# Decode attention on one core: a third halving on VectorE for half of each tile, and the Values matmuls in a hardware loop on TensorE

## The chip, the core and the metric

The kernel runs on one core of a Trainium2 chip. Five engines work side by side[...]: TensorE (PE, matmuls into PSUM), VectorE (DVE), ScalarE (ACT), GpSimd (POOL) and SyncE (SP), which here issues the loads. Sixteen DMA engines carry the loads. The metric is the time on the device in microseconds (us).

## The reference

One query per head attends to 4,096 keys: 8 batches of 32 heads, head dimension D = 128, all in bfloat16.

```python
B, H, Sq, Skv, Dh = 8, 32, 1, 4096, 128
def reference(q, k, v):
    scale = q.shape[-1] ** -0.5
    scores = jnp.einsum('bhqd,bhkd->bhqk', q, k) * scale
    attn = _softmax(scores, axis=-1)
    return jnp.einsum('bhqk,bhkd->bhqd', attn, v)
```

K and V are 268 MB each, and every element is used once.

## The kernel before

**Tiles.** A tile is 8 heads; there are 32 tiles (NT). One tile of K or V is 128 partitions x 256 positions (C) x 128 (D) in bfloat16, 8.39 MB. Sixteen partitions hold one head, each with 256 of its positions.

**Scores of a tile.** `q_prep` (lines 156 to 168) spreads the queries of the 8 heads over the partitions, with two small matmuls and two copies on ScalarE. `product` (170) works on units of 64 positions, four to a tile: VectorE multiplies K by the query in place (175), then adds the upper half of D to the lower (178), so that 64 of 128 remain. `sum_over_d` (185) lets PE add these up: with an identity as weights, eight matmuls of 512 columns accumulate into one bank of PSUM, each taking 8 values of D (DS) for 64 positions. `scores_of` (199) reduces the last 8 on VectorE. `weights_of` (209) finds the maximum and a bias per head (212 to 223), and ScalarE computes the eight exponentials (231), one for each head, with the row sums. For each head, the bias outside its own 16 partitions is so low that the weights there are zero.

**Values.** `values_of` (241) multiplies the weights by V: 64 matmuls (256), each with 4 positions x 8 heads = 32 columns of weights and 4 x 128 = 512 columns of V. They go round four groups of 32 output rows (`group`, TG = 4). `copy_of` (280) brings the result from PSUM to SBUF on ScalarE; `result_of` (289) picks the matching rows and sums them on PE (301), two tiles into one bank; `norm_of`, `recip_of` and `finish_of` divide by the sum and store. Every eight tiles, ScalarE issues an output DMA.

**Buffers.** K has two buffers, V has one (`KB, VB = 2, 1`). The last tile's V uses a K buffer. A load into a buffer waits until the last reader of the former tile is done: for V that is the last Values matmul, for K the last matmul of `sum_over_d`.

**Order.** Everything stands in the order in which the program is written (`manual_schedule`). In iteration t, SP gets the load of K of t + 1 and then V of t. PE gets the sums of units 0 and 1 of tile t, then the Values of tile t - 1, then the sums of units 2 and 3, then the pick of t - 1. VectorE gets the four units in turn, each unit's last reduce one unit later, and the maxima at the end. For the last two tiles the Values stand behind all four sums. Each engine takes its instructions strictly in this order.

**Cuts.** Some loads are issued in pieces (`cuts`, line 131): K of tile 0 as a quarter, a quarter and a half, with the load of the queries behind the first quarter; K of the last four tiles in halves (or a quarter, a quarter and a half), V of the last tile in seven pieces.

Of the kernel before, what the change touches and what calls it, by code (L numbers as in the profile page):

```python
# [7 lines left out]
ACT = mybir.ActivationFunctionType  # L8
ALU = mybir.AluOpType
AX = mybir.AxisListType  # L10
BF16 = mybir.dt.bfloat16
F32 = mybir.dt.float32

G = 8
KB, VB = 2, 1
TG = 4
R = 2
OB = 4
LAST = 4
NEG = -1.0e30  # L20


@with_exitstack
def kernel(
# [7 lines left out]
    nc = tc.nc  # L32
    B, H, Sq, D = q.shape
    S = k.shape[2]
    P = nc.NUM_PARTITIONS
# [3 lines left out]
    C = S // PH  # L39
    NT = NH // G  # L40
    scale = float(D) ** -0.5
    UC = 64
    DS = 512 // UC
    NU = C // UC
    MC = UC
    CB = 4
    RG = R * G
    NQ = NT // R
    TB = 32
    AG = CB * G  # L50
    assert TG * AG == P and NH % P == 0 and P % G == 0 and TB % PH == 0 and C % CB == 0

    q_n = q.rearrange("b h o d -> (b h o) d").rearrange("(x p) d -> p x d", p=P)
# [13 lines left out]
    ps_v = ctx.enter_context(tc.tile_pool(name="ps_v", bufs=2, space=bass.MemoryType.PSUM))  # L67
# [42 lines left out]
    for j in range(TG):  # L110
# [17 lines left out]
    nc.gpsimd.memset(w_last[:], 0.0)  # L128

    loads = {}  # L130
    cuts = {
        ("k", 0): [C // 4, C // 4, C // 2],
        ("k", NT - 4): [C // 2] * 2,
        ("k", NT - 3): [C // 2] * 2,
        ("k", NT - 2): [C // 2] * 2,
        ("k", NT - 1): [C // 4, C // 4, C // 2],
# [3 lines left out]
    def load(kind, t):  # L140
        src = k_t if kind == "k" else v_t
        home = "v" if kind == "v" and t < NT - 1 else "k"
        pool = k_pool if home == "k" else v_pool
        buf = pool.tile([P, C, D], BF16, name=f"{kind}t", tag=home)
        c0 = 0
        for n in cuts.get((kind, t), [C]):
            nc.sync.dma_start(buf[:, c0 : c0 + n, :], src[t, :, c0 : c0 + n, :])  # L147
            c0 += n
            if kind == "k" and t == 0 and c0 == n:
                nc.sync.dma_start(q_all[:], q_n)  # L150
        assert c0 == C
        loads[kind, t] = buf
# [3 lines left out]
    def q_prep(t):  # L156
        x, p0 = divmod(t * G, P)
        qh = ps_q.tile([G, D], F32, name="qh", tag="qp")
        nc.tensor.matmul(  # L159
            qh[:], lhsT=ident[:, p0 : p0 + G], rhs=q_all[:, x, :], start=True, stop=True  # L160
        )
        qg = q_pool.tile([G, D], BF16, name="qg", tag="qg")
        nc.scalar.activation(out=qg[:], in_=qh[:], func=ACT.Copy)  # L163
        qp = ps_q.tile([P, D], F32, name="qp", tag="qp")
        nc.tensor.matmul(qp[:], lhsT=heads[:].rearrange("g h x -> g (h x)"), rhs=qg[:], start=True, stop=True)  # L165
        qb = q_pool.tile([P, 1, D], BF16, name="qb", tag="qb")
        nc.scalar.activation(out=qb[:, 0, :], in_=qp[:], func=ACT.Copy)  # L167
        qbs[t] = qb

    def product(t, lo, hi):  # L170
        kt = loads["k", t]
        qb = qbs[t]
        for c0 in range(lo, hi, MC):
            part = kt[:, c0 : c0 + MC, :]
            nc.vector.tensor_tensor(  # L175
                out=part, in0=part, in1=qb[:].to_broadcast([P, MC, D]), op=ALU.mult
            )
            nc.vector.tensor_tensor(  # L178
                out=part[:, :, 0 : D // 2], in0=part[:, :, 0 : D // 2],
                in1=part[:, :, D // 2 : D], op=ALU.add,  # L180
            )

    sums = {}

    def sum_over_d(t, u):
        kt = loads["k", t]
        ps = ps_s.tile([P, UC, DS], F32, name="ps", tag="ps")
        n = D // 2 // DS
        for s in range(n):
            nc.tensor.matmul(  # L190
                ps[:], lhsT=ident[:],
                rhs=kt[:, u * UC : (u + 1) * UC, s * DS : (s + 1) * DS],
                start=(s == 0), stop=(s == n - 1),
            )
        sums[t, u] = ps
# [3 lines left out]
    def scores_of(t, u):  # L199
        if u == 0:  # L200
            scs[t] = sc_pool.tile([P, C], F32, name="sc", tag="sc")
        nc.vector.tensor_reduce(  # L202
            out=scs[t][:, u * UC : (u + 1) * UC], in_=sums.pop((t, u))[:], axis=AX.X, op=ALU.add
        )

    ws = {}
# [30 lines left out]
            nc.gpsimd.tensor_copy(out=w_last[:, :, RG - G : RG], in_=w[:, C - LAST : C, :])  # L237

    avs = {}

    def values_of(t, lo, hi):
        vt = loads["v", t]
        w = ws[t]
        if lo == 0:
            avs[t] = ps_v.tile([P, CB * D], F32, name="av", tag="av")
        end = C if t < NT - 1 else C - LAST


        group = [
            0 if t == NT - 1 and C // 2 <= c0 < 3 * C // 4 else c0 // CB % TG  # L250
            for c0 in range(0, end, CB)
        ]
        for c0 in range(lo, hi, CB):
            i = c0 // CB
            j = group[i]
            nc.tensor.matmul(  # L256
                avs[t][j * AG : (j + 1) * AG, :], lhsT=w[:, c0 : c0 + CB, :],
                rhs=vt[:, c0 : c0 + CB, :], start=(i < TG), stop=(j not in group[i + 1 :]),
            )

    ops = {}
# [4 lines left out]
    def norm_of(n):  # L266
        zp = ps_z.tile([RG, 1], F32, name="zp", tag="zp")
        nc.tensor.matmul(  # L268
            zp[:], lhsT=esums.pop(n).rearrange("p r g -> p (r g)"), rhs=ones[:],
            start=True, stop=True,  # L270
        )
        zps[n] = zp

    def recip_of(n):
        rzs[n] = small.tile([RG, 1], F32, name="rz", tag="rz")
        nc.vector.reciprocal(out=rzs[n][:], in_=zps.pop(n)[:])  # L276
# [3 lines left out]
    def copy_of(t):  # L280
        comb = small.tile([P, CB, D], BF16, name="comb", tag="comb")
        av = avs.pop(t)[:].rearrange("p (m d) -> p m d", d=D)
        n = CB if t < NT - 1 else CB // 2
        nc.scalar.activation(out=comb[:, 0:n, :], in_=av[:, 0:n, :], func=ACT.Copy)  # L284
        if n < CB:
            nc.vector.tensor_copy(out=comb[:, n:CB, :], in_=av[:, n:CB, :])  # L286
        combs[t] = comb

    def result_of(t):
        n, r = divmod(t, R)  # L290
        comb = combs.pop(t)
        if r == 0:
            ops[n] = ps_o.tile([RG, D], F32, name="op", tag="op")
        if t == NT - 1:
            for i in range(LAST):
                nc.tensor.matmul(
                    ops[n][:], lhsT=w_last[:, i, :], rhs=loads["v", t][:, C - LAST + i, :],
                    start=False, stop=False,
                )
        for m in range(CB):  # L300
            nc.tensor.matmul(  # L301
                ops[n][:], lhsT=pick[:, m, r, :], rhs=comb[:, m, :],
                start=(r == 0 and m == 0), stop=(r == R - 1 and m == CB - 1),
            )

    def finish_of(n):
        s, u = divmod(n, OB)
        if u == 0:
            stages[s] = o_pool.tile([RG, OB, D], BF16, name="stage", tag="stage")
        nc.scalar.activation(  # L310
            out=stages[s][:, u, :], in_=ops.pop(n)[:], func=ACT.Copy, scale=rzs.pop(n)[:, 0:1]
        )
        last = s == NQ // OB - 1
        if u == OB - 1 or (last and u == OB - 2):
            lo = u if (last and u == OB - 1) else 0
            nc.scalar.dma_start(o_n[s, :, lo : u + 1, :], stages[s][:, lo : u + 1, :])

    Q = C // 4
    load("k", 0)
    with tc.manual_schedule():  # L320
        q_prep(0)
        for t in range(NT):
            v_last = t >= NT - 2
            n = t // R - 1
            if t + 1 < NT:
                load("k", t + 1)
            load("v", t)
            product(t, 0, Q)
            sum_over_d(t, 0)
            if t > 2 and t % R == 1:  # L330
                recip_of(n)
                finish_of(n)
            if t + 1 < NT:
                q_prep(t + 1)
            product(t, Q, 2 * Q)
            sum_over_d(t, 1)
            scores_of(t, 0)
            if t > 0 and not v_last:
                values_of(t - 1, 0, C)
                copy_of(t - 1)  # L340
            product(t, 2 * Q, 3 * Q)
            sum_over_d(t, 2)
            scores_of(t, 1)
            product(t, 3 * Q, C)
            sum_over_d(t, 3)
            scores_of(t, 2)
            if t > 0 and v_last:
                values_of(t - 1, 0, C)
            scores_of(t, 3)
            weights_of(t)  # L350
            if t > 0:
                if v_last:
                    copy_of(t - 1)
                if t % R == 0:
                    norm_of(n)
                result_of(t - 1)
        values_of(NT - 1, 0, C // 2)
        norm_of(NQ - 1)
        recip_of(NQ - 1)
        values_of(NT - 1, C // 2, C - LAST)  # L360
        copy_of(NT - 1)
        result_of(NT - 1)
        finish_of(NQ - 1)

# [29 lines left out]
```

## Time and profile before

| what | value |
|---|---|
| median of 10 runs | 1254.55 us (1254.4 to 1254.77) |
| the profiled execution | 1254.51 us, span 1252.8 us |
| bytes read | 536.94 MB, 429 GB/s over the span |
| VectorE busy | 967.5 us (77%) |
| PE matmuls busy | 550.7 us (44%) |
| ScalarE busy | 343.3 us (27%) |
| granted TensorE clock, mean | 0.688 |
| instruction fetches on queue q8 | 26 packets, 0.43 MB |

The span runs from the first to the last instruction of the core. In a line of groups, the columns are line, engine, operation, output and inputs, shapes, count, then the busy time in us and the mean ns of one, then the engine's idle time ahead of them and what ended most of it. In a line of the timeline, the start and the duration come first, and the bracket gives the idle time before and its releaser. In the chain of work that ended last, each line has start, duration and what ran or was waited for. PE's clock is granted by a throttle: 1.00 is full speed.

### The profile page before, as it was taken

The numbers are of one execution on the slowest core, as the hardware profiler recorded it, in microseconds if no ns is written. First come the engines' busy times: TensorE is split into PE (matmuls) and PEld (weight loads), VectorE is DVE, ScalarE is ACT, GpSimd is POOL, SyncE is SP. The second block draws the span as 40 slices with busy tenths as digits, with TensorE's granted clock in tenths as the row PEclk, the third lists the DMA queues.
The fourth block names the chain that finished last, engine by engine and source line by source line (L and its number), as shares of the span: only waits on it lengthen the run. The fifth ranks groups of instructions, "written<-read, shape, count | busy, mean of one in ns | idle before, by whom it ended". The sixth has DMA issues, their size and how long they took to land.

```text
span 1252.8 us, 8134 instructions
## 1 busy us (share of the span) xinstructions
PE 550.7 (44%) x3299; PEld 201.3 (16%) x3299; DVE 967.5 (77%) x531; ACT 343.3 (27%) x625; POOL 6.0 (0%) x26
## 2 busy tenths in 40 slices
PE   2444543445533355333554344543345424544355
PEld 0111111111111111111111111111111101111112
DVE  6877887777977779777797777886778877977981
ACT  0333123332133321333213333123330233321333
POOL 1000000000000000000000000000000000000000
PEclk9966756776666676667675667656677566766677
DMA  9999999999999999999999999999999999999997
GB/s 404 435 436 432 434 435 435 434 432 432 435 434 431 434 432 427 435 434 433 432 434 434 432 436 435 434 434 435 429 427 433 432 435 434 423 426 433 429 440 311
DMA packets 11734, 537.53 MB, mean 429 GB/s; under 512 B 1840, under 2 KB 2096, under 8 KB 2352
## 3 DMA queue, kind: packets, MB, share of 16 engines
q1 hardware_dynamic: 11360, 536.94, 99.3%
q8 instruction: 26, 0.43, 0.1%
q10 hardware_dynamic: 336, 0.07, 0.0%
q14 instruction: 12, 0.10, 0.0%
HBM read 536.94 MB, written 0.07 MB: 429 GB/s over the span
## 4 chain that ended last, share of the span: by engine, by line
DMA 79%; PE 15%; DVE 6%; issue 0%; another core or an unknown queue 0%; ACT 0%; SPq 0%
DMA vt<-in_v_dram 78%; PE av L256 13%; DVE kt L175 3%; DVE kt L178 2%; PE ps L190 1%; DMA q_all<-in_q_dram 1%; DVE sc L202 0%; SPq L147 0%; DVE pmax L212 0%; DVE spread L214 0%; DVE nmax L219 0%; DVE comb L286 0%; ACT comb L284 0%; ACT stage L310 0%
## 5 line engine op out<-in xcount | busy, mean ns | idle before, releaser
L175 DVE TENSOR_TENSOR kt<-kt,qb 128x8192 bf16<-128x8192 bf16 x128 | 565.1, 4415 | 185.2 <-DMA kt<-in_k_dram 178.5
L190 PE MATMUL ps<-kt,ident 128*128 128x512 bf16 x1024 | 351.8, 506 | 573.3 <-DVE kt L178 573.3
L231 ACT ACTIVATE w<-sc,bias 128x256 bf16<-128x256 f32 x256 | 300.5, 1587 | 255.4 <-DVE bias L223 255.4
L178 DVE TENSOR_TENSOR kt<-kt 128x4096 bf16<-128x4096 bf16 x128 | 293.3, 2292 | 4.4
L190 PEld LDWEIGHTS <-ident 128*128 128x128 bf16 x1024 | 118.9, 118 | 776.5 <-issue 502.7
L256 PE MATMUL av<-vt,w 128*32 128x512 bf16 x2047 | 175.6, 510 | 88.3 <-DMA vt<-in_v_dram 88.3
L202 DVE TENSOR_REDUCE sc<-ps 128x64 f32<-128x512 f32 x128 | 87.6, 685 | 65.6 <-PE ps L190 65.6
L284 ACT ACTIVATE comb<-av 128x512 bf16<-128x512 f32 (+1 forms) x32 | 19.5, 609 | 415.3 <-PE av L256 415.3
L231 ACT ACTIVATION_READ_ACCUMULATOR w<-sc,bias 128x1 f32 x256 | 126.5, 494 | 0.0
L256 PEld LDWEIGHTS <-w 128*32 128x32 bf16 x2047 | 68.3, 124 | 204.7 <-DMA vt<-in_v_dram 107.2
L163 ACT ACTIVATE qg<-qh 8x128 bf16<-8x128 f32 x32 | 8.5, 267 | 167.8 <-PE qh L159 167.8
L310 ACT ACTIVATE stage<-op,rz 16x128 bf16<-16x128 f32 x16 | 6.0, 372 | 57.5 <-DVE rz L276 42.8
L301 PE MATMUL op<-comb,pick 128*16 128x128 bf16 x128 | 13.1, 226 | 16.5 <-ACT comb L284 16.1
L212 DVE TENSOR_REDUCE pmax<-sc 128x1 f32<-128x256 f32 x32 | 13.4, 420 | 1.1
L165 PE MATMUL qp<-qg,heads 8*128 8x128 bf16 x32 | 7.6, 238 | 12.7 <-ACT qg L163 12.7
L276 DVE RECIPROCAL rz<-zp 16x1 f32<-16x1 f32 x16 | 2.4, 149 | 14.0 <-PE zp L268 14.0
L159 PE MATMUL qh<-q_all,ident 128*8 128x128 bf16 x32 | 8.2, 256 | 8.5 <-DMA q_all<-in_q_dram 8.5
L167 ACT ACTIVATE qb<-qp 128x128 bf16<-128x128 f32 x32 | 8.9, 278 | 10.4 <-PE qp L165 10.4
L301 PEld LDWEIGHTS <-pick 128*16 128x16 bf16 x128 | 7.5, 90 | 24.2 <-issue 24.0
L214 DVE TENSOR_SCALAR spread<-same,pmax 128x32 f32<-128x32 f32 x32 | 7.7, 241 | 1.1
L223 DVE TENSOR_SCALAR bias<-own,nmax 128x8 f32<-128x8 f32 x32 | 7.4, 231 | 1.1
L219 DVE TRANSPOSE_TENSOR_REDUCE nmax<-spread 128x1 f32<-128x32 f32 x32 | 6.8, 212 | 1.1
(27 smaller groups left out, 20.2 us busy)
## 6 DMA issues: line engine op xcount, KB each, us to landing
kt<-in_k_dram SPq DMA_DIRECT2D x8, 4096.0 KB, 43.5
kt<-in_k_dram SPq DMA_DIRECT2D x4, 2048.0 KB, 22.8
vt<-in_v_dram SPq DMA_DIRECT2D x1, 4096.0 KB, 41.7
vt<-in_v_dram SPq DMA_DIRECT2D x1, 2048.0 KB, 46.2
vt<-in_v_dram SPq DMA_DIRECT2D x1, 1024.0 KB, 48.1
vt<-in_v_dram SPq DMA_DIRECT2D x1, 512.0 KB, 48.9
vt<-in_v_dram SPq DMA_DIRECT2D x31, 33.4
kt<-in_k_dram SPq DMA_DIRECT2D x27, 47.4
```

Source lines behind the costliest of these rows:

```text
L159: nc.tensor.matmul(qh[:], lhsT=ident[:, p0 : p0 + G], rhs=q_all[:, x, :], start=True, stop=True)
L163: nc.scalar.activation(out=qg[:], in_=qh[:], func=ACT.Copy)
L167: nc.scalar.activation(out=qb[:, 0, :], in_=qp[:], func=ACT.Copy)
L175: nc.vector.tensor_tensor(out=part, in0=part, in1=qb[:].to_broadcast([P, MC, D]), op=ALU.mult)
L178: nc.vector.tensor_tensor(out=part[:, :, 0 : D // 2], in0=part[:, :, 0 : D // 2], in1=part[:, :, D // 2 : D], op=ALU.add,)
L190: nc.tensor.matmul(ps[:], lhsT=ident[:], rhs=kt[:, u * UC : (u + 1) * UC, s * DS : (s + 1) * DS], start=(s == 0), stop=(s == n - 1),)
L202: nc.vector.tensor_reduce(out=scs[t][:, u * UC : (u + 1) * UC], in_=sums.pop((t, u))[:], axis=AX.X, op=ALU.add)
L212: nc.vector.tensor_reduce(out=pmax[:], in_=sc[:], axis=AX.X, op=ALU.max)
L231: nc.scalar.activation(out=w[:, :, g], in_=sc[:], func=ACT.Exp, bias=bias[:, g : g + 1], scale=scale, accum_out=esum[:, t % R, g : g + 1],)
L256: nc.tensor.matmul(avs[t][j * AG : (j + 1) * AG, :], lhsT=w[:, c0 : c0 + CB, :], rhs=vt[:, c0 : c0 + CB, :], start=(i < TG), stop=(j not i ...
L284: nc.scalar.activation(out=comb[:, 0:n, :], in_=av[:, 0:n, :], func=ACT.Copy)
L301: nc.tensor.matmul(ops[n][:], lhsT=pick[:, m, r, :], rhs=comb[:, m, :], start=(r == 0 and m == 0), stop=(r == R - 1 and m == CB - 1),)
```

## The change

Four edits are made.

1. For units 0 and 1 of each tile up to tile 28, VectorE adds once more, so that 32 of 128 values of D remain, and PE takes four matmuls for such a unit instead of eight (`width_of`).
2. K of tile 0 is loaded in two halves, with the queries behind the first half; K of tile 28 (NT - 4) is loaded in one piece.
3. The last copy out of PSUM is done by ScalarE alone; before, ScalarE and VectorE took half each. In the last tile, 12 instead of 16 matmuls of the second half go to row group 0.
4. The Values of tiles 0 to 30 are computed by `values_loop`: two matmuls, then a hardware loop on PE of ten rounds with six matmuls each whose addresses come from registers, then two more. All 64 go to one group of 32 rows. The loop is a critical section: PE waits at its entry for what stands ahead of it in the program, and drains at its end. The copy and the pick read 32 partitions instead of 128. The loads of K of t + 1 and V of t, and the products, are ordered behind the loop that precedes them; this orders the program and adds no semaphore.

```diff
-        ("k", 0): [C // 4, C // 4, C // 2],
-        ("k", NT - 4): [C // 2] * 2,
+        ("k", 0): [C // 2] * 2,
...
+    def width_of(t, u):
+        return D // 4 if u < NU // 2 and t < NT - 3 else D // 2
...
+            if width_of(t, c0 // UC) < D // 2:
+                nc.vector.tensor_tensor(
+                    out=part[:, :, 0 : D // 4], in0=part[:, :, 0 : D // 4],
+                    in1=part[:, :, D // 4 : D // 2], op=ALU.add,
+                )
...
-        n = D // 2 // DS
+        n = width_of(t, u) // DS
...
+    def values_loop(t):
+        vf = loads["v", t][:].rearrange("p c d -> p (c d)")
+        wf = ws[t][:].rearrange("p c g -> p (c g)")
+        avs[t] = ps_v.tile([P, CB * D], F32, name="av", tag="av")
+        av = avs[t][0:AG, :]
+        nv, nw = CB * D, CB * G
+        def one(i, **how):
+            pe.matmul(
+                av, lhsT=wf[:, i * nw : (i + 1) * nw], rhs=vf[:, i * nv : (i + 1) * nv], **how
+            )
+        with tc.tile_critical() as loop:
+            for i in range(EDGE):
+                one(i, start=(i == 0), stop=False)
+            end = (NV - EDGE) * nw
+            pe.reg_mov(rw, EDGE * nw)
+            pe.reg_mov(rv, EDGE * nv)
+            with pe.While(lambda: pe.snap(rw, min_val=EDGE * nw, max_val=end) < end):
+                ow = pe.snap(rw, min_val=EDGE * nw, max_val=end - LOOP * nw)
+                ov = pe.snap(rv, min_val=EDGE * nv, max_val=(NV - EDGE - LOOP) * nv)
+                for i in range(LOOP):
+                    pe.matmul(
+                        av, lhsT=wf[:, bass.ds(ow + i * nw, nw)],
+                        rhs=vf[:, bass.ds(ov + i * nv, nv)],
+                        start=False, stop=False,
+                    )
+                pe.reg_add(rw, rw, LOOP * nw)
+                pe.reg_add(rv, rv, LOOP * nv)
+            for i in range(NV - EDGE, NV):
+                one(i, start=False, stop=(i == NV - 1))
+        loops.append(loop)
...
-            0 if t == NT - 1 and C // 2 <= c0 < 3 * C // 4 else c0 // CB % TG
+            0 if t == NT - 1 and C // 2 <= c0 < C // 2 + 3 * C // 16 else c0 // CB % TG
...
-        n = CB if t < NT - 1 else CB // 2
-        nc.scalar.activation(out=comb[:, 0:n, :], in_=av[:, 0:n, :], func=ACT.Copy)
-        if n < CB:
-            nc.vector.tensor_copy(out=comb[:, n:CB, :], in_=av[:, n:CB, :])
+        n = P if t == NT - 1 else AG
+        nc.scalar.activation(out=comb[0:n, :, :], in_=av[0:n, :, :], func=ACT.Copy)
...
+    def before_values(t):
+        v_last = t >= NT - 2
...
+        product(t, Q, 2 * Q)
+        sum_over_d(t, 1)
+        scores_of(t, 0)
+        if v_last:
+            products_end(t)
...
+    def after_values(t):
...
+        if t > 0 and not v_last:
+            copy_of(t - 1)
+        if t + 1 < NT:
+            load("k", t + 1)
+        load("v", t)
+        if not v_last:
+            products_end(t)
+        scores_of(t, 3)
+        weights_of(t)
...
         for t in range(NT):
...
             if t > 0:
+                after_values(t - 1)
+            before_values(t)
+            if t > 0:
+                values_loop(t - 1)
+        after_values(NT - 1)
```

`NV` is 64, `EDGE` 2 and `LOOP` 6. `products_end` holds the units 2 and 3 with their sums and reduces.

More of the change, by code (lines that the diff above doesn't have):

```diff
@@ L19 @@
 LAST = 4
+LOOP = 6
+EDGE = 2
 NEG = -1.0e30
@@ L50 @@
     AG = CB * G
+    NV = C // CB
+    assert (NV - 2 * EDGE) % LOOP == 0
     assert TG * AG == P and NH % P == 0 and P % G == 0 and TB % PH == 0 and C % CB == 0
@@ L130, with behind_loop @@
     loads = {}
+    loops = []
+    def behind_loop(made):
+        if loops:
+            tc.add_manual_dep(
+                made.ins, loops[-1].name,
+                mybir.DependencyInfo(
+                    mybir.DependencyClass.NoSync, mybir.DependencyReason.SCHED_ONLY
+                ),
+            )
     cuts = {
-        ("k", 0): [C // 4, C // 4, C // 2],
-        ("k", NT - 4): [C // 2] * 2,
+        ("k", 0): [C // 2] * 2,
         ("k", NT - 3): [C // 2] * 2,
@@ L146, in load @@
         for n in cuts.get((kind, t), [C]):
-            nc.sync.dma_start(buf[:, c0 : c0 + n, :], src[t, :, c0 : c0 + n, :])
+            dma = nc.sync.dma_start(buf[:, c0 : c0 + n, :], src[t, :, c0 : c0 + n, :])
+            behind_loop(dma)
             c0 += n
@@ L174, in product @@
             part = kt[:, c0 : c0 + MC, :]
-            nc.vector.tensor_tensor(
+            made = nc.vector.tensor_tensor(
                 out=part, in0=part, in1=qb[:].to_broadcast([P, MC, D]), op=ALU.mult
             )
+            behind_loop(made)
             nc.vector.tensor_tensor(
@@ L239 @@
     avs = {}
+    pe = nc.tensor
+    rv = pe.alloc_register("rv")
+    rw = pe.alloc_register("rw")
+    def values_loop(t):
[22 more added lines that the diff above has]
+                        start=False, stop=False,
+                    )
+                pe.reg_add(rw, rw, LOOP * nw)
[3 more added lines that the diff above has]
+        loops.append(loop)
     def values_of(t, lo, hi):
@@ L299, in result_of @@
                 )
+        e = P if t == NT - 1 else AG
         for m in range(CB):
             nc.tensor.matmul(
-                ops[n][:], lhsT=pick[:, m, r, :], rhs=comb[:, m, :],
+                ops[n][:], lhsT=pick[0:e, m, r, :], rhs=comb[0:e, m, :],
                 start=(r == 0 and m == 0), stop=(r == R - 1 and m == CB - 1),
@@ L318, with products_end @@
     Q = C // 4
+    def before_values(t):
+        v_last = t >= NT - 2
+        n = t // R - 1
+        if t == 0:
+            q_prep(0)
+        product(t, 0, Q)
+        sum_over_d(t, 0)
+        if t > 2 and t % R == 1:
+            recip_of(n)
+            finish_of(n)
+        if t + 1 < NT:
+            q_prep(t + 1)
+        product(t, Q, 2 * Q)
[3 more added lines that the diff above has]
+            products_end(t)
+    def products_end(t):
+        product(t, 2 * Q, 3 * Q)
+        sum_over_d(t, 2)
+        scores_of(t, 1)
+        product(t, 3 * Q, C)
+        sum_over_d(t, 3)
+        scores_of(t, 2)
@@ L319 @@
+    def after_values(t):
+        v_last = t >= NT - 2
+        if t > 0 and not v_last:
+            copy_of(t - 1)
+        if t + 1 < NT:
+            load("k", t + 1)
[5 more added lines that the diff above has]
+        if t > 0:
+            if v_last:
+                copy_of(t - 1)
+            if t % R == 0:
+                norm_of(t // R - 1)
+            result_of(t - 1)
     load("k", 0)
-    with tc.manual_schedule():
-        q_prep(0)
+    E = mybir.EngineType
@@ L322 @@
+    with tc.manual_schedule(engines={E.PE, E.DVE, E.Activation, E.SP}):
         for t in range(NT):
[L323 to L350, printed above, removed]
-            if t > 0:
[L352 to L356, printed above, removed]
+            if t > 0:
+                after_values(t - 1)
@@ L357 @@
+            before_values(t)
+            if t > 0:
+                values_loop(t - 1)
+        after_values(NT - 1)
         values_of(NT - 1, 0, C // 2)
```

## The prediction

> **What bounds the kernel now.** I read the page's shares first, then the chain that ended last in order of time, then one period of the timeline, then clock and durations of single stretches. The page:
>
> ```profile
> span 1252.8 us, 8134 instructions
> DMA  9999999999999999999999999999999999999997
> HBM read 536.94 MB, written 0.07 MB: 429 GB/s over the span
> DMA 79%; PE 15%; DVE 6%; issue 0%; another core or an unknown queue 0%; ACT 0%; SPq 0%
> L256 PE MATMUL av<-vt,w 128*32 128x512 bf16 x2047 | 175.6, 510 | 88.3 <-DMA vt<-in_v_dram 88.3
> q8 instruction: 26, 0.43, 0.1%
> ```
>
> The transfers are full in every slice; chain and bytes agree that K and V set the time. The chain in order of time shows how it closes, once per tile:
>
> ```profile
> 567.78 5.35 PE av L256 x64
> 573.15 33.50 DMA vt<-in_v_dram
> 606.66 0.04 issue
> 606.70 6.50 PE av L256 x63
> 613.21 32.01 DMA vt<-in_v_dram
> 645.22 0.04 issue
> 645.27 5.35 PE av L256 x64
> ```
>
> Period 645.27 - 606.70 = 38.6 us, two 8.39 MB loads. V has one buffer, so a V load can be issued only when the Values of the tile before are done; it then still waits some 32 us, most of it queued behind the K load. That queueing is the cover. K and V take 19.3 us each, so after V lands at 606.7 the next K lands at 626 and only then is the next V needed, about 2 us of issue ahead: Values may end as late as 624 and end at 613.2. The compute of one period:
>
> ```profile
> 606.70 6.46 PE L256 MATMUL av<-vt,w 128*32 128x512 bf16 x64 [2.42 <-DMA vt<-in_v_dram]
> 613.09 1.90 PE L190 MATMUL ps<-kt,ident 128*128 128x512 bf16 x8
> 618.85 0.23 DVE L223 TENSOR_SCALAR bias<-own,nmax 128x8 f32<-128x8 f32 x1
> 625.97 4.43 DVE L175 TENSOR_TENSOR kt<-kt,qb 128x8192 bf16<-128x8192 bf16 x1 [6.88 <-DMA kt<-in_k_dram]
> 630.43 2.29 DVE L178 TENSOR_TENSOR kt<-kt 128x4096 bf16<-128x4096 bf16 x1
> 632.77 3.57 PE L190 MATMUL ps<-kt,ident 128*128 128x512 bf16 x8 [15.34 <-DVE kt L178]
> ```
>
> VectorE has only 6.9 us of slack before K. Clock in stretches (columns: stretch, length, PE busy, granted clock, DMA share, GB/s):
>
> ```profile
> 606.70:613.10 6.40, 6.40 (x65) 0.55 1.06 461
> 1193.00:1196.50 3.50, 3.50 (x67) 1.00 1.04 445
> 613.10:615.00 1.90, 1.89 (x12) 1.00 1.04 448
> 593.99:597.50 3.51, 3.51 (x9) 0.50 0.95 411
> ```
>
> At full clock 64 Values take 3.5 us (55 ns each) but eight L190 matmuls, also 512 columns, take 1.90 us (216 ns each after the tail), 3.5 us at half clock: the 64 Values run four abreast.
>
> [...]
>
> **The change, part by part.**
>
> *Values loop (31 tiles).* All 64 matmuls go to one 32-row group, so nothing runs abreast: 64 x 0.216 = 13.8 us at full clock against 3.5. Cold start: Values now take 5.2 to 6.5 us against 3.5, so half clock adds 1.7 to 3.0; I take 2.0. [...] Register work: seven address instructions and one move an iteration, unpriced. [...] Let X be the loop's time[...].
>
> *What X feeds.* In PE's order, sums of the second half of the same tile stand behind the loop. From loop end E: drain 0.3, sixteen L190 at full clock 3.65, last reduce, maxima and bias to the next product 1.87 (1193.04 to 1194.91 in the timeline): E + 5.8. Then the first half of the next tile's products: 6.67 per unit now (625.97 to 632.64), plus the new halving of 2,048 elements, half of L178's 4,096: 1.17, so 2 x 7.84 = 15.7: E + 21.5. Four cold sums 1.88 and the entry's waits 0.1: the next loop starts at E + 23.5. So a period is **X + 23.5**, and it beats the transfers' 38.7 from X = 15.2 up. At 17.4 it is 40.9. V independently needs E + 2 + 19.4 = E + 21.4, just inside. ScalarE's exps (9.4 us after bias) are inside too. The four sums fewer per unit save 1.7 us on this path; the halving costs 2.3: net +0.6, included. The other four sums saved lie beside the products.
>
> *Entry waits.* The loop waits for all that stands ahead of it in the program: mostly long done, but in tiles 9, 17 and 25 also an output DMA that ScalarE issues after its exps at about E + 15.6, which lands 14.3 us later (its row of issues), so 6.4 late. Behind it are the loop, the sums and VectorE's reduce. 3 x 6.4 = 19 us (0 if it lands quickly).
>
> *Start.* K's first load in halves is 4.19 MB ahead of q_all instead of 2.1: q_all lands 4.85 us later and the first product starts at 14.6 instead of 9.7. Tile 0 also halves twice (2.3): the first loop starts at 68.1, against 61.8. Were transfers still the limit, this would be hidden behind K0, K1, V0 (58 us); with computing the limit it counts.
>
> *End.* Tiles 29 to 31 keep the old halving. After loop 28's end E: products of tile 30 27.9 us from E + 5.8, sums 3.4, loop 29 from E + 37.3. Only its end frees V's buffer, when K31 has long landed; V30 lands 21.5 later; loop 30 starts at E + 58.8 + X and ends X later; the rest of tile 31, output included, about 10: E + 68.8 + 2X = E + 103.6.
>
> *Beside other work or nothing.* [...] The copy of 32 rows streams the same columns (0.62 us), on ScalarE's idle time. The last copy whole: 0.62 for 0.39 + 0.44, 0.2 saved; last tile's group 12 matmuls wide instead of 16: about 0.6 saved. K28 in one piece instead of halves: hidden while computing is behind.
>
> **Sum**, against the profiled execution: 68.1 + 28 x 40.9 + 17.4 + 103.6 + 19 = 1353 us of span. Launch around the span adds 1.7 (1254.51 against 1252.8; the median of the runs, 1254.55, is the same): **1355**. Every us of X is worth 31.
>
> **Rivals.** (1) *A slow loop.* Register instructions or a clock that stays half while only a quarter of the columns work: X = 20 to 28, 1355 + 31 x 2.6 = 1436 to 1684. For: no such instruction is in this trace, and the granted clock was 0.55 through 606 to 613. Against: it rose to 1.00 in bursts of continuous work. (2) *Transfers stay the limit.* If X is at most 15.2 the period stays 38.7. Then only the end shows: loop 28 ends 9 us later than now, loop 29 takes 14 instead of 3.6, V30 is issued at 1216 instead of 1197 while K31 lands at 1208: 10 us idle, 1256 to 1272. Against: it needs 13.8 plus almost no cold time. (3) *Faster.* 26 instruction blocks become about 14[...]. If all of them went through one of the 16 DMA engines, 12 x 16 KiB at 27 GB/s free it 7 us: 1247 to 1250. It decides only if the loop stays within 15.2 and V30's gap is covered, which the end argues against; the 0.1% of all engines says less than 1 us if spread.
>
> **Chances.** X between 15.2 and 20, transfers no longer the limit: 0.56 (own range 1285 to 1436). Slow loop: 0.30, of it 0.08 above 1610. Transfers the limit, paying at the end: 0.07. No measurable change: 0.02. Faster: 0.05. About 0.2% is what a measurement of this kernel can tell from no change. The range 1262 to 1610 holds the first case, most of the second and part of the third. Faster 0.05, same 0.02, slower 0.93.
>
> **What would show it.** Right: the chain mostly PE and VectorE; the loop's line near 17 us per tile, matmuls 216 ns or more apart; VectorE waiting on PE's sums instead of K; DMA below 9 in the slices; loop starts 41 us apart, 47 in tiles 9, 17 and 25; fewer instruction packets. Wrong: a loop under 15 us with VectorE still waiting for K (rival 2 or 3), or matmuls over 300 ns apart (rival 1). A loop whose matmuls overlap, or sums that need not queue behind it, would undo the argument.

## The result and the profile after

| | before | after |
|---|---|---|
| median of the runs | 1254.52 us (1254.37 to 1255.89) | 1358.4 us (1355.7 to 1360.86) |
| ratio, 95% interval | | 1.0828 [1.0818, 1.0837] |
| the profiled execution | 1254.51 us, span 1252.8 us | 1355.1 us, span 1353.4 us |
| rate over the span | 429 GB/s | 397 GB/s |
| granted TensorE clock, mean | 0.688 | 0.769 |

The kernel is 8.3% slower; the execution that the profiler took was the fastest of its ten. On the page of the changed kernel, the lines that answer to those shown of before:

```profile
span 1353.4 us, 11319 instructions
...
DMA  9989999999998999999997999999999899999683
...
q8 instruction: 14, 0.23, 0.1%
HBM read 536.94 MB, written 0.07 MB: 397 GB/s over the span
...
L217 PE MATMUL ps<-kt,ident 128*128 128x512 bf16 x792 | 253.7, 476 | 483.3 <-DVE kt L205 427.8
L294 PE MATMUL av<-vt,w 128*32 x1860 | 457.9, 403 | 3.3
```

The transfers are no longer full in every slice; instruction blocks fell from 26 to 14; the Values' line, which had waited 88.3 us for V, shows no wait for V any more (run 5 tells why that is not quite the whole story). The page's chain of what ended last is of no use here: it goes back only to the drain of the last loop. The period has to be read from the timeline of PE (start, duration, what; in brackets the idle time before and its releaser):

```profile
640.84 1.04 PE L280 MATMUL av<-vt,w 128*32 128x512 bf16 x2 [0.44 <-issue]
641.67 14.78 PE L294 MATMUL av<-vt,w 128*32 x60
656.51 0.61 PE L280 MATMUL av<-vt,w 128*32 128x512 bf16 x2
657.31 3.61 PE L217 MATMUL ps<-kt,ident 128*128 128x512 bf16 x16 [0.20 <-PEq L284]
660.85 0.39 PE L364 MATMUL op<-comb,pick 32*16 32x128 bf16 x4
670.86 1.86 PE L217 MATMUL ps<-kt,ident 128*128 128x512 bf16 x4 [9.62 <-DVE kt L205]
672.65 0.27 PE L175 MATMUL qh<-q_all,ident 128*8 128x128 bf16 x1
673.34 0.26 PE L181 MATMUL qp<-qg,heads 8*128 8x128 bf16 x1 [0.41 <-ACT qg L179]
678.78 1.86 PE L217 MATMUL ps<-kt,ident 128*128 128x512 bf16 x4 [5.18 <-DVE kt L205]
681.08 1.04 PE L280 MATMUL av<-vt,w 128*32 128x512 bf16 x2 [0.44 <-issue]
```

The Values take 640.84 to 657.11, 16.3 us where they took 5.3 to 6.5 in the tiles shown of before; the next loop starts 24.0 us after that end. VectorE in the same period:

```profile
650.70 2.29 DVE L200 TENSOR_TENSOR kt<-kt 128x4096 bf16<-128x4096 bf16 x1
659.23 0.69 DVE L229 TENSOR_REDUCE sc<-ps 128x64 f32<-128x512 f32 x1 [6.24 <-PE ps L217]
...
662.80 4.42 DVE L196 TENSOR_TENSOR kt<-kt,qb 128x8192 bf16<-128x8192 bf16 x1
667.26 2.29 DVE L200 TENSOR_TENSOR kt<-kt 128x4096 bf16<-128x4096 bf16 x1
669.58 1.22 DVE L205 TENSOR_TENSOR kt<-kt 128x2048 bf16<-128x2048 bf16 x1
```

Its wait moved: 6.9 us for K before, 6.2 us for PE's sums now, and the next product starts without any wait.

Time after against time before, by parts: the first loop starts 6.9 us later (68.66 against 61.8), the stretch from first to 29th Values takes 1148.7 us instead of 1088.3, the 29th Values take 10.1 us longer (16.27 against 6.13), and from there to the end it is 119.7 us instead of 96.6.

### The profile page after: what moved, and what is told of

Its sections match the earlier page's. It is cut to its first block, busy times and chain, and to the rows that moved or that the text cites. A ratio compares the mean times of both kernels' runs of the same rounds, so it can differ in the third digit from the quotient of the medians.

```text
span 1353.4 us, 11319 instructions
## 1 busy us (share of the span) xinstructions
PE 788.2 (58%) x3067; PEld 298.5 (22%) x3067; DVE 1038.1 (77%) x588; ACT 341.4 (25%) x625; POOL 6.0 (0%) x26
## 5 line engine op out<-in xcount | busy, mean ns | idle before, releaser
L217 PE MATMUL ps<-kt,ident 128*128 128x512 bf16 x792 | 253.7, 476 | 483.3 <-DVE kt L205 427.8
L294 PE MATMUL av<-vt,w 128*32 x1860 | 457.9, 403 | 3.3
L294 PEld LDWEIGHTS av<-vt,w 128*32 x1860 | 188.4, 101 | 279.2 <-issue 119.6
L217 PEld LDWEIGHTS <-ident 128*128 128x128 bf16 x792 | 85.5, 110 | 620.9 <-issue 568.7
L348 ACT ACTIVATE comb<-av 32x512 bf16<-32x512 f32 (+1 forms) x32 | 18.8, 587 | 738.0 <-PEq L284 731.9
L280 PE MATMUL av<-vt,w 128*32 128x512 bf16 x124 | 50.8, 502 | 48.1 <-DMA out_dram<-stage 17.9
L205 DVE TENSOR_TENSOR kt<-kt 128x2048 bf16<-128x2048 bf16 x58 | 71.0, 1224 | 2.0
L340 DVE RECIPROCAL rz<-zp 16x1 f32<-16x1 f32 x16 | 2.4, 150 | 39.5 <-PE zp L332 39.5
L280 PEld LDWEIGHTS av<-vt,w 128*32 128x32 bf16 x124 | 7.7, 101 | 90.4 <-issue 89.8
L364 PE MATMUL op<-comb,pick 32*16 32x128 bf16 (+1 forms) x128 | 12.3, 215 | 1.7 <-ACT comb L348 1.7
L364 PEld LDWEIGHTS <-pick 32*16 32x16 bf16 (+1 forms) x128 | 6.7, 83 | 9.0 <-issue 8.6
## 6 DMA issues: line engine op xcount, KB each, us to landing
vt<-in_v_dram SPq DMA_DIRECT2D x1, 512.0 KB, 39.5
vt<-in_v_dram SPq DMA_DIRECT2D x31, 22.1
```

Of the source, the lines that this page charges most:

```text
L205: nc.vector.tensor_tensor(out=part[:, :, 0 : D // 4], in0=part[:, :, 0 : D // 4], in1=part[:, :, D // 4 : D // 2], op=ALU.add,)
L217: nc.tensor.matmul(ps[:], lhsT=ident[:], rhs=kt[:, u * UC : (u + 1) * UC, s * DS : (s + 1) * DS], start=(s == 0), stop=(s == n - 1),)
L280: pe.matmul(av, lhsT=wf[:, i * nw : (i + 1) * nw], rhs=vf[:, i * nv : (i + 1) * nv], **how)
L294: pe.matmul(av, lhsT=wf[:, bass.ds(ow + i * nw, nw)], rhs=vf[:, bass.ds(ov + i * nv, nv)], start=False, stop=False,)
L348: nc.scalar.activation(out=comb[0:n, :, :], in_=av[0:n, :, :], func=ACT.Copy)
L364: nc.tensor.matmul(ops[n][:], lhsT=pick[0:e, m, r, :], rhs=comb[0:e, m, :], start=(r == 0 and m == 0), stop=(r == R - 1 and m == CB - 1),)
```

## The experiments

**1. Is it the loop, or the work added on VectorE?** Everything of the change but the loop:

```diff
-                values_loop(t - 1)
+                values_of(t - 1, 0, C)
```

(with the copy and the pick over 128 partitions again).

> Everything of the change except the hardware loop: the Values are again 64 static matmuls that go round four groups of 32 rows; the smaller adds, the cuts and the last copy stay changed. Theory (the loop's length and what queues behind it on PE set the time): Values take 5 to 6.5 us, the period is the transfers' 38.7 us again, the 2.4 us of added halving and the later start of the first product vanish in VectorE's wait for K (6.9 us before), and the time is 1252 to 1258 us. Rival (the added halving on VectorE carries a good part of the loss): 58 adds of 1.22 us stay, 71 us, so the time stays above 1300 us.

Measured: 1253.07 us, ratio to before 0.9988 [0.9981, 0.9995]. The 58 added adds cost nothing; the loss of 104 us is all the loop's, with its one group of rows and its order. The median is even a little below that of before, which runs 8 to 11 follow up.

**2. The groups or the loop's instructions?** The same 64 matmuls, unrolled, all into one group:

```diff
-            0 if t == NT - 1 and C // 2 <= c0 < C // 2 + 3 * C // 16 else c0 // CB % TG
+            0 if t < NT - 1 or C // 2 <= c0 < C // 2 + 3 * C // 16 else c0 // CB % TG
...
-                values_loop(t - 1)
+                values_of(t - 1, 0, C)
```

> As changed, but the Values of tiles 0 to 30 are 64 static matmuls into one group of 32 rows: no loop, no registers, no waits at an entry, no drain. Theory (four abreast was lost, and that is most of the loop's 16.3 us): Values take 8 x 0.43 + 56 x 0.216 = 15.5 us, the period is 15.5 + 23.4 = 38.9 us, the output transfer no longer holds the Values up (18 us), the end loses its 12 us wait for GpSimd, but V of tile 30 is still late: 1265 to 1285 us. Rival (register and branch instructions make the loop long, the row groups do not matter): Values take 5 to 7 us and the time is 1252 to 1260 us.

Measured: 1283.44 us, ratio 1.0228 [1.0211, 1.0245]. The timeline of PE of this kernel:

```profile
618.38 15.91 PE L320 MATMUL av<-vt,w 128*32 128x512 bf16 x64 [1.00 <-DMA vt<-in_v_dram]
634.22 3.63 PE L217 MATMUL ps<-kt,ident 128*128 128x512 bf16 x16
...
658.00 14.88 PE L320 MATMUL av<-vt,w 128*32 128x512 bf16 x64 [0.43 <-DMA vt<-in_v_dram]
```

The 30 runs of Values take 14.0 to 16.5 us, median 15.4: the loop's length is there without a loop. Four abreast was lost, as expected, and without a loop that costs 29 us. Of the remaining 75 us, the loop's own length explains less than 1 us a tile, some 28 us in all; most of the rest lies in its entry waits and at the end (runs 6 and 7).

**3. What do the loop's own instructions cost?** Each matmul in the loop takes 128 of 512 columns, about a quarter of the array's work (at full clock the four 128-column matmuls of L364 stand 0.056 us apart in the changed kernel, those of 512 columns 0.216); three quarters of those columns are left out of the result.

```diff
-                        av, lhsT=wf[:, bass.ds(ow + i * nw, nw)],
-                        rhs=vf[:, bass.ds(ov + i * nv, nv)],
+                        av[:, 0:D], lhsT=wf[:, bass.ds(ow + i * nw, nw)],
+                        rhs=vf[:, bass.ds(ov + i * nv, D)],
```

> As changed, but each of the 60 matmuls inside the loop takes 128 of its 512 columns of V; three quarters of the Values' columns inside the loop are left out. This measures what the loop's own instructions cost, since the array needs only 54 ns per matmul at full clock. Theory A (the last rounds of the loop are paced by PE's sequencer at 1.50 us for six): ten rounds of about 1.5 us, the loop still takes 14 to 16 us and the time falls by no more than 70 us, to 1290 to 1350 us. Theory B (the array alone sets the loop, the 1.50 us per round is something else): the loop takes 4 to 7 us and the time is 1255 to 1285 us.

Measured: 1413.03 us, ratio 1.1263 [1.124, 1.1285]. Less work, and 55 us slower than the changed kernel: neither theory had that. The timeline of PE:

```profile
626.88 1.04 PE L280 MATMUL av<-vt,w 128*32 128x512 bf16 x2 [0.43 <-issue]
627.71 0.85 PE L294 MATMUL av<-vt,w 128*32 x6
629.00 1.05 PE L294 MATMUL av<-vt,w 128*32 x6 [0.45 <-issue]
630.51 1.05 PE L294 MATMUL av<-vt,w 128*32 x6 [0.45 <-issue]
632.01 1.05 PE L294 MATMUL av<-vt,w 128*32 x6 [0.45 <-issue]
...
642.65 1.03 PE L280 MATMUL av<-vt,w 128*32 128x512 bf16 x2 [0.55 <-issue]
643.87 4.98 PE L217 MATMUL ps<-kt,ident 128*128 128x512 bf16 x16 [0.19 <-PEq L284]
```

Rounds stand 1.506 us apart whatever the array does, here as in the last rounds of the changed kernel. In most rounds the trace has 0.70 us across the back edge, 0.195 us to the second matmul and then 0.152 us from one to the next. Theory A holds for the length, if not to the figure: the loop takes 16.7 us (median) where it said 14 to 16, 0.4 more than with whole matmuls. What made the time grow stands behind the loop. The windows of this kernel (stretch, length, PE busy, granted clock, DMA share, GB/s):

```profile
626.90:642.60 15.70, 11.11 (x62) 0.50 0.78 338
643.90:648.80 4.90, 4.90 (x17) 0.72 1.13 428
```

In this tile the clock stayed at 0.50 through the loop, as in 17 of its 30 loops; in the other 13, full clock came for 3.5 us at most. So the sixteen sums behind the loop took 4.98 us here and 6.12 in the tile before, against 3.61. In the changed kernel the clock is 1.00 from 645 to 651, and 67 to 93% of every loop runs at full clock. Whether the gaps or the narrower matmuls kept the clock down, no run separates. So two things limit the loop of the changed kernel, nearly level: the array needs 14 to 16.5 us (run 2), the sequencer ten rounds of 1.506 us and some 1.2 us for the static ends, 16.3, and 16.3 it is in most tiles.

**4. Fewer rounds.** Eight matmuls a round, seven rounds (`LOOP = 8`, `EDGE = 4`).

> As changed, but the loop has eight matmuls a round and seven rounds, with four static matmuls ahead and four behind. If a round's fixed part (a compare, two branches' worth of jumps, the register updates) is what lifts six matmuls from 1.30 to 1.50 us, three rounds fewer save at most 3 x 0.2 us of the loop: 15.7 to 16.2 us for the Values, 5 to 18 us off the time, 1340 to 1353 us. If each matmul's own address instruction paces the loop at 0.25 us, a round takes 2.0 us and the time is within 4 us of the change's 1358 us.

Measured: 1343.53 us (1335.73 to 1349.42), ratio 1.0688 [1.0636, 1.074]. The Values now take 14.5 to 16.9 us, median 15.7: the back edge was worth 0.6 us, and the length varies as it does unrolled. From run 3, a round of eight should need 1.506 + 2 x 0.152 = 1.81 us of sequencer, an estimate, and 8 x 0.216 = 1.73 us of array; the trace has 1.73 us. That is 15 us off the time, as the first reading had it. The four executions fall in two pairs (1336 to 1338 us and 1349), and the trace is of the slower pair.

**5. Does the added halving lie on the chain?** The loop without the third halving, with the loads cut as before.

```diff
-        return D // 4 if u < NU // 2 and t < NT - 3 else D // 2
+        return D // 2
```

> The loop, its order and the last copy as changed, but without the third halving, and with the loads cut as before the change. Theory (VectorE's added halving lies on the chain from one loop to the next: two adds of 1.22 us against 1.71 us of sums saved on PE): each period is 0.7 us shorter, 28 x 0.7 = 20 us, and the first loop starts at 62 instead of 68.7: 27 us less than the change's 1358, 1326 to 1336 us. Rival (the halving lies beside PE's work and helps by taking eight matmuls a tile off PE): the time stays or grows, 1352 to 1375 us.

Measured: 1358.73 us, ratio 1.0833 [1.0816, 1.085]: the same as the changed kernel. The theory as put is refuted. The first loop does start 5.7 us earlier (63.0), but the stretch from first to 29th Values takes 1155.9 us, 7.1 more. VectorE's chain did become shorter, but the loops still start a median 24.5 us after the end of the one before:

```profile
654.60 0.33 SPq L163 DMA_DIRECT2D vt<-in_v_dram  x1
678.99 1.03 PE L281 MATMUL av<-vt,w 128*32 128x512 bf16 x2 [2.80 <-DVE kt L197]
```

V's load is issued by SP 0.2 us after the loop's end and takes 23.3 us to land. In the trace, V lands at 637.1 and 677.9 us, and the first matmul of the loop starts at 638.17 and 678.99: 1.1 us behind V, both times. The releaser in the bracket misleads, since VectorE's product was long under way; in every period but the three with an output transfer, the loop starts 1.1 to 1.2 us behind V's landing. So there are two rings of nearly equal length around the loop: over VectorE, and over V's one buffer. To test that, half of V's load was taken away from this kernel as well; this leaves out half of V:

```diff
+        some = [C // 2 + CB // 2] if home == "v" else [C]
-        for n in cuts.get((kind, t), [C]):
+        for n in cuts.get((kind, t), some):
...
-                        rhs=vf[:, bass.ds(ov + i * nv, nv)],
+                        rhs=vf[:, bass.ds(ov + i * nv // 2, nv)],
```

(the static matmuls and the register step likewise).

> The loop without the third halving, but of each V tile (all but the last) only 130 of 256 positions are loaded, and the matmuls of the loop read overlapping windows of them; the other V is left out. PE, VectorE and ScalarE keep all their instructions. Theory (without the halving, the next loop waited for V, whose load is issued when the loop before ends and lands 23 us later, plus 1.1 us from landing to the first matmul): V lands early, VectorE's chain of 22.9 us from one loop's end to the next start is left, all ordinary periods are 39.2 us, and the time falls by 28 x 1.5 = 40 us, to 1300 to 1325 us. Rival (the loops start 24 us apart for another reason, such as the clock or the order on PE): the periods stay at 40.7 us and the time above 1345 us.

Measured: 1312.18 us, ratio 1.0459 [1.044, 1.0478].

```profile
635.34 0.60 PE L282 MATMUL av<-vt,w 128*32 128x512 bf16 x2
658.99 0.60 PE L282 MATMUL av<-vt,w 128*32 128x512 bf16 x2 [0.43 <-issue]
```

From end to start it is now 23.0 us (median), most periods are 39.1 to 39.5 us, and V lands 8 us or more ahead of every loop. With the halving, VectorE's ring takes 24.0 us. So the halving does cost on that ring, and taking it out only hands the time to V's ring.

V's ring binds in the changed kernel too: of its 25 periods without an output transfer, seven start 1.1 us behind V's landing (24.2 to 24.6 us after the loop before), the other 18 start 1.6 to 2.1 us behind it.

**6. The output transfer at the entry.** The stores are issued behind the next loop:

```diff
+            made = nc.scalar.dma_start(o_n[s, :, lo : u + 1, :], stages[s][:, lo : u + 1, :])
+            if n < NQ - 1:
+                behind_loop(made)
```

> As changed, but the output transfers, all but the last, are issued behind the next loop instead of ahead of it, so that no loop waits for one at its entry. Theory: the three periods of 45.6 to 45.9 us become 40.4, and the last loop no longer has that transfer among its waits either, where it was hidden: 16 us less, 1340 to 1345 us. Rival (the long periods come from something else in every eighth tile): three long periods stay, 1354 to 1362 us.

Measured: 1332.71 us, ratio 1.062 [1.0601, 1.064]: 25.7 us less, nearly 10 more than expected. In the changed kernel the waits say

```profile
PE av L280 <- DMA out_dram<-stage: 17.9, 3, 6.1
...
PE av L280 <- POOL w_last L264: 12.0, 1, 12.0
```

and here both lines are gone. The three long periods (45.6 to 45.9 us) became 40.3 to 42.2, and from loop 29's end to loop 30's start it is 27.9 us instead of 37.4. The store behind the last loop is followed, in ScalarE's order, by the exponentials of tile 31. Before, they stood ahead of loop 30 in the built order, and with them GpSimd's copy of the last weights; loop 30 waited for both without needing either.

**7. The end.** The Values of tiles 29 and 30 static in four groups, the loop for the other 29 tiles.

```diff
-            if t > 0:
+            if 0 < t < NT - 2:
                 values_loop(t - 1)
+            elif t > 0:
+                values_of(t - 1, 0, C)
```

> As changed, but the Values of tiles 29 and 30 are static and go round four groups, as before the change; the loop stays for tiles 0 to 28. Theory (the end of the changed kernel, 119.7 us from the end of loop 28 where it was 96.6 before, is long because loop 29 frees V's buffer late, VectorE waits for the sum of exponentials behind that loop, and loop 30 waits for tile 31's weights and GpSimd's copy of them): the Values of tile 29 take 3.6 us, V of tile 30 is issued 13 us earlier, the last loads set the end, and the last loop ends at the same time as now: 1326 to 1336 us. Rival (the end is long because the last loads come late anyway): at most 12 us less, 1346 us or more.

Measured: 1333.22 us, ratio 1.0626 [1.0607, 1.0644]: 25 us less, as the theory had it. From loop 28's end it is 95.1 us to the end (1238.33 to 1333.4); before the change it was 96.6. In the changed kernel, VectorE shows where two of its pieces were:

```profile
1277.23 2.29 DVE L200 TENSOR_TENSOR kt<-kt 128x4096 bf16<-128x4096 bf16 x1
1289.62 0.16 DVE L340 RECIPROCAL rz<-zp 16x1 f32<-16x1 f32 x1 [10.10 <-PE zp L332]
1289.70 4.39 DVE L196 TENSOR_TENSOR kt<-kt,qb 128x8192 bf16<-128x8192 bf16 x1
```

The reciprocal needs a sum that PE makes behind loop 29, and three units of tile 31's products stand behind the reciprocal.

**8 to 11. Where the 1.5 us of run 1 come from.** The difference is small, and each of these four kernels counts as the same as before within 2%. The third edit alone, on the kernel before:

> The kernel before with the third edit alone: the last copy whole on ScalarE, and 12 instead of 16 matmuls of the last tile in row group 0. The change without its loop was 1.5 us faster than the kernel before. If that came from the last copy and the group, at the very end where nothing covers them, this is as fast: 1253.0 to 1253.6 us, ratio 0.9985 to 0.9993. If it came from fewer instructions to fetch or from the cuts, this stays at 1254.5 us, ratio 0.9996 to 1.0004.

Measured: 1254.38 us, 0.9998 [0.999, 1.0007]: no gain. With the cuts added:

> The kernel before with the second and third edits: first K in halves, K of tile 28 whole, the last copy whole, 12 matmuls in the last group; no third halving, no loop. The third edit alone gained nothing (0.9998), the three edits together 1.5 us. If the cuts are the cause: 1252.8 to 1253.5 us. If it is the halving, with two fewer blocks of PE instructions to fetch: 1254.2 to 1254.7 us.

Measured: 1254.18 us, 0.9997 [0.9989, 1.0005]: none either. That leaves the halving, which takes 464 instructions off PE. More of it, without the loop (`u < NU - 1` for `u < NU // 2`):

> The change without its loop, and the third halving on three of the four units of each tile up to tile 28. VectorE gets 1.2 us more a tile, of the 4 us that it still waits for K; PE has some 230 instructions less. If fewer instruction blocks save time: 1252.2 to 1253.0 us, below the 1253.07 us of two units. If not: 1253.0 to 1253.6 us. If VectorE becomes the limit: above 1256 us.

Measured: 1253.04 us, 0.9988 [0.9982, 0.9995]: no further gain, though blocks of PE instructions fell from 24 to 23. And the reverse, the change without its loop but with 512 more PE instructions in a gap:

```diff
+        for _ in range(9):
             nc.tensor.matmul(
                 qh[:], lhsT=ident[:, p0 : p0 + G], rhs=q_all[:, x, :], start=True, stop=True
             )
```

> The change without its loop, with the small matmul that gathers a tile's queries repeated nine times into the same place: 16 more PE instructions a tile, 512 in all, 0.9 us of PE in a gap of over 5 us; nothing waits for them that is on the path. PE's instructions come to 26 blocks again, from 24. If the 1.5 us that the change without its loop gains come from two blocks fewer, the gain goes: 1254.0 to 1254.6 us. If the halving gains in another way, it stays: 1252.8 to 1253.4 us.

Measured: 1254.3 us, 0.9998 [0.999, 1.0006]; 26 blocks. The gain is gone. The chain in order of time, without the added instructions and then with them:

```profile
1240.18 3.41 PE av L320 x29
1243.63 4.21 PE av L320 x30
1247.86 0.61 ACT comb L348
```

```profile
1199.39 48.78 DMA vt<-in_v_dram
1248.16 0.04 issue
1248.21 0.69 PE av L321 x3
```

With 26 blocks the end waits for the last piece of V; with 24 V is there in time (the last load completes at 1247.5 us against 1248.8) and PE's own last matmuls end the kernel, which fits that 23 blocks bring nothing more. The trace tells a load's landing in sixteen parts. In all four kernels with 26 blocks (before, runs 8, 9 and 11) one part of the last load lands 1.3 to 1.6 us behind the other fifteen; with 24 and 23 blocks it is 0.3 at most. So the step looks like one block ahead of one part, rather than the bytes of two; no run moved a block by itself. The best version measured is the change without its loop: 1253.04 to 1253.07 us against 1254.5, 0.12%, at the edge of what can be told.

## Why the prediction was right, and where it was not

The forecast of 1355 us met 1355.1 for the profiled execution and 1358.4 for the median, but three of its terms missed. The mechanism was right in the main; that the sum came within 1 us of the span was luck, since 16.6 us too much in the periods and the loop met 16.1 too little at the end:

| term of the sum | predicted | measured |
|---|---|---|
| start of the first loop | 68.1 | 68.66 |
| 28 periods, waits for the output included | 28 x 40.9 + 19 = 1164.2 | 1148.7 |
| loop 28 | 17.4 | 16.27 |
| from its end to the end | 103.6 | 119.7 |
| span | 1353 | 1353.4 |

**Right, and shown.** Four abreast is lost (run 2: 14.0 to 16.5 us for the 64 Values). The next tile's work stands behind the loop on PE and VectorE, so that the transfers stop being the limit. The output transfer holds up the loops that stand in tiles 9, 17 and 25: three waits, 17.9 us in all against 19 predicted. The first K load in halves moves the first product to 14.4 us (14.6 predicted). The added halving hides beside K when there is no loop (run 1), and costs on VectorE's ring when there is one (run 5). 14 instruction blocks were predicted and came.

**The loop's length, mis-sized: 17.4, measured 16.3.** The step added a cold start of 2.0 us and ten back edges to 13.8 us; for the back edges it had a figure that nothing of before showed. The two do not add. Matmuls run 0.427 us apart at half clock, slower than the sequencer's 0.25 (1.506 us for six), so it runs ahead meanwhile: in the loop that starts at 640.84, the first compare-and-branch starts at 642.35, when two of the round's six matmuls have started. The loads of weights show no longer gap at the first six back edges than between other matmuls (0.28 us at half clock, 0.12 at full), and 0.47 to 0.55 us at the last three. The back edge itself, 0.70 us in run 3, has in the trace of the changed kernel a compare-and-branch of 0.17 us and a second branch of 0.07; the rest is register work and gaps, which no run separates.

**The rest of the period, mis-sized: 23.5, measured 24.0.** With a loop of 16.3 that makes a median period of 40.4 us, not 40.9. The halving took 1.22 us, not 1.17, the drain left PE idle for 0.20, not 0.3, and the entry took 0.44, not 0.1. And V's ring was put at 21.4 us; it is 23.0 to 24.6 (0.2 us to the issue, 22.1 median from issue to landing, 23.0 to 23.3 where it binds, and 1.1 from landing to the first matmul; 22.1 is 2.8 more than a load's half of the 38.6 us period of before, where about 2 was put). The reading "V is just inside" was true by 0.5 to 1.0 us in 18 periods, and false in seven. The claim that the halving costs 0.6 us net was therefore near on its ring (24.0 against 23.0 us, run 5) and wrong for the time: without it nothing was gained.

**The end: 16 us missed.** The step let VectorE run on into tile 31 and took only an output transfer among the entry waits. Two waits were overlooked: the reciprocal behind loop 29 (10.1 us), and tile 31's weights and GpSimd's copy ahead of loop 30 (12.0 us). They lie on one chain and do not add: from loop 29's end to loop 30's start it took 37.4 us where 21.5 were predicted. The second follows from the very rule the prediction stated, that the loop waits for all that stands ahead of it, but in the built order, not in the source's.

**Rivals.** The slow loop was excluded: 16.3 us, clock 1.00 from the tenth matmul or so in the tile shown. Run 3 shows how near it was: the same loop with less work stayed at half clock in most tiles. Transfers as the limit did not come about. The faster rival's premise, that instruction blocks cost more than their bytes, held in small (1.2 us for two blocks in runs 1 and 11, where an even spread over 16 engines would be 0.08), but the loop buries it. That all blocks use one DMA engine is unlikely: a block is one packet of about 1 us, 26 of them on one engine would put one part of a load far behind the others, and in run 11 no load's parts land more than 6.4 us apart. In the changed kernel each of the seven V loads that bind has its last part 0.9 to 1.4 us behind the fifteenth, and a block fetched within 7 us of its issue; of the other 18 loads two had a block so near, and none had a part over 0.4 us late. That makes a block the likely cause of the late V; no run tests it.

## What to carry to other kernels

A queueing delay is cover only for as long as the work under it fits: ask, for each buffer that a lengthened step frees, which ring it closes, add the ring up from end to start, and look for the second ring that is within 1 us of the first, since removing one only exposes the other. A critical section waits for everything that was built ahead of it, needed or not (here 17.9 us for output transfers and 12.0 for the last weights); list that from the built order, and keep stores and other tiles' work behind it (run 6: 25.7 us less).

## What the runs showed of the hardware

A loop round on TensorE with six matmuls whose addresses come from registers took 1.506 us with 128 columns a matmul (run 3) and, in the last rounds of the changed kernel, with 512: 0.152 us for most of the narrow ones, 0.70 us across the back edge. Through a stretch of narrow matmuls with gaps of 0.45 us the granted clock stayed at 0.50 for all of its 15.7 us, and so in 17 of 30 loops, and the work behind it paid: less work in the loop made the kernel 55 us slower. With two 16 KB blocks of instructions more (26 against 24, runs 13 and 1), the last load landed 1.3 us later, and of its sixteen parts only one.
